# Maxima of the second pair in two rows, another rate of maxima in the first pairs, and routing and list operands in fewer instructions set further apart

## The chip, the cores and the metric

The kernel runs on one core of one Trainium2 chip. The metric is device time in microseconds of one execution. A core has a matrix engine (PE, with its weight loads PEld), a vector engine (DVE), an activation engine (ACT), a general engine (POOL) and a queue engine (SP) that here only issues transfers. Each of them works through its own queue in order. Matmuls write to PSUM, which DVE and ACT empty; POOL cannot read PSUM.

## The reference

Attention with pairs of queries averaged, then a mixture of eight experts in which each token goes to one expert.

```python
B, H, S, D = 8, 8, 1152, 64
q_pool = q.reshape(B, H, S // 2, 2, D).mean(axis=3)            # 576 queries a head
scores = 1 / sqrt(D) * q_pool @ k.T
attn = exp(scores - scores.max(-1)); attn /= attn.sum(-1) + 1e-9
x = (attn @ v) as (4608 tokens, 512)
logits = x @ w_gate + modality_bias[modality_id]               # 8 experts
e_idx = argmax(logits); gate_w = softmax(logits)[e_idx]
for e in range(8):
    mask = e_idx == e
    out[mask] = gate_w[mask] * (relu(x[mask] @ w1[e]) @ w2[e]) # 512 -> 1024 -> 512
```

## The kernel before, in words

**Attention.** 64 heads are taken as 32 pairs p (two batches of one head number). A pair is 18 steps t (`NSTEP`), so attention is 576 steps, and the order of every engine's queue (PE, ACT, DVE, POOL) is written by the loop over t: `ORD` says for each step, in turn modulo three, which generators move on. `s` advances the scores of a third of a head (four banks of 432 columns, two matmuls each, L833 and L834, an exponential on ACT, L835, tile Pe). `v` advances the products with the values (L886 to L888, tile xp), which trail by `LAG` steps. `M` and `X` advance the maxima pass (`maxpass`) of a later pair: PE multiplies a block of 128 queries by 512 keys into a PSUM tile pm (L771), DVE reduces it to one column of mp (L772); the last 128 keys of up to four blocks share one tile (L779, L780). When all nine blocks of 128 queries are done, `row` reduces mp to nine columns (m9, L743), PE turns them (L747), DVE scales them (mr, L756) and SP copies them as one row into B2 (L757), where the scores find them. `maxpass` has 21 stops and a last turn that ends it, 22 turns. `M` comes three times in three steps, `X` once per step: it gives three turns before step `T_F` = 7, one in each step up to 53, then one in every fourth step, or one whenever two passes are queued. Pair 1's pass is queued at step `T_M1`, pair p's at `T_MAX` = -24 before its own first step, for pair 2 six steps later (`D2`).

For each pair the queue also carries: the sum of the query halves (rawq, POOL, L603), the high and low fp16 parts of queries and keys (qh, hi, lo), their copies into QB, B1 and B2 (SP), the low parts Pl of the exponentials (L816 on ACT, L818 on DVE, two thirds on one and one third on the other; `LOWS_LIST` gives ACT some more in pairs 26 to 30), the power of two that scales the values (`power`, `scales`: half, sc and the two scale tiles scales and both, L696 and L698), the scaled values VH (L725, POOL from pair 2 on), VS (L735, DVE), vl (L723), the result of a head (rs, rr, x, L904 to L909) and its split for the gate's logits. `V1`, `T_P1`, `T_P2`, `D2` place such work of pairs 1 and 2.

**Routing.** After every eighth pair one of four token groups g has its logits. `route(g)` is a generator of small instructions on DVE and POOL: the one-hot of the best expert, its gate, and with ten small matmuls each token's position in its expert. `yield n` lets n steps pass. It stands in the list `side`, which moves at the end of a step. After group 2 the generator `first_list` makes the list of the first six blocks of 256 tokens: `first_blocks` (which expert owns a block), `place` (row of each token), `listing` with `operands` (DVE builds ol, o and r for nine tiles of tokens in three portions, PE multiplies them, L498). At step 557 whatever is left of it is run at once (`gather_first`), and POOL gathers the first rows. In steps that are not forced the generator waits `SLOW` = 3 steps between portions.

**Experts.** Blocks of 256 tokens, weights split into two fp16 parts, three products each; group 3's route and the second list run beside them, one `yield` per eighth of a product.

Of the kernel before, what the change touches and what calls it, by code (L numbers as in the profile page):

```python
# [13 lines left out]
I32 = mybir.dt.int32  # L14
# [29 lines left out]
RS = 2  # L44
# [27 lines left out]
V1 = (7, 9, (12, 13), 14, (14, 15))  # L72
# [70 lines left out]
T_PRE = 2  # L143
# [11 lines left out]
class Router:  # L155
# [11 lines left out]
    def setup(self, ids, w_gate, bias):  # L167
        nc, con = self.nc, self.con
        wg = con.tile([P, 4, E], F32, name="wg")
        nc.sync.dma_start(out=wg, in_=w_gate.rearrange("(c p) e -> p c e", p=P))  # L170
        self.wg = con.tile([P, 4, 3, E], BF16, name="wg3")
        for i in range(3):
            nc.gpsimd.tensor_copy(self.wg[:, :, i], wg)
            if i < 2:
                nc.gpsimd.tensor_tensor(wg, wg, self.wg[:, :, i], op=ALU.subtract)
        self.b0 = con.tile([P, 2, E], F32, name="bias")
        nc.sync.dma_start(out=self.b0, in_=bias.rearrange("m e -> (m e)").unsqueeze(0).broadcast_to([P, 2 * E]).rearrange("p (m e) -> p m e", m=2))
        idt = con.tile([P, NTT, 2], I32, name="idt")
# [10 lines left out]
        self.ie = self.iota("ie", E)  # L189
        self.lane16 = con.tile([P, P], BF16, name="lane16")  # L190
# [76 lines left out]
    def route(self, g, eng):  # L267

        nc, sm = self.nc, self.sm
# [20 lines left out]
        yield RS  # L290
# [6 lines left out]
        yield RS  # L297
        oh = big[1][:, 1]
        nc.vector.tensor_tensor(oh, key, bc(kmin), op=ALU.is_equal)
        oh16 = sm.tile([P, NT, E], BF16, name="oh16")  # L300
        nc.vector.tensor_copy(oh16, oh)
        nc.vector.tensor_single_scalar(self.exp[:, ts], kmin, float(E), op=ALU.add)
        yield RS
        sx = sm.tile([P, NT], F32, name="sx")
        nc.vector.tensor_reduce(sx, w, op=ALU.add, axis=AX.X)
        nc.vector.tensor_single_scalar(sx, sx, EPS, op=ALU.add)
# [3 lines left out]
        nc.vector.tensor_single_scalar(ts2[:, 0:1], ts2[:, 0:1], 1.0 / XSC, op=ALU.mult)  # L310
# [5 lines left out]
        yield RS  # L316
# [102 lines left out]
    def place(self, nt, late):  # L419
# [23 lines left out]
        if late:  # L443
# [18 lines left out]
        nc.vector.tensor_copy(self.hi, ri)  # L462
        nc.vector.tensor_single_scalar(self.hi, self.hi, -float(2 * T // P), op=ALU.add)

    def operands(self, g, n, out):

        nc, sm = self.nc, self.sm
        for q in range(3):
            ts = slice(g * NT + 3 * q, g * NT + 3 * q + 3)
            ol = sm.tile([P, 3, P], BF16, name=f"ol{q}", bufs=1 + self.lag)  # L470
            nc.vector.tensor_tensor(ol, self.lo[:, ts].unsqueeze(2).broadcast_to([P, 3, P]), self.lane16.unsqueeze(1).broadcast_to([P, 3, P]),
                                    op=ALU.is_equal)
            yield SLOW
            o = sm.tile([P, 3, n], F32, name=f"o{n}")
            r = sm.tile([P, 3, 2, n], BF16, name=f"r{n}_{q}", bufs=1 + self.lag)
            nc.vector.tensor_tensor(o, self.hi[:, ts].unsqueeze(2).broadcast_to([P, 3, n]), self.col[:, 0:n].unsqueeze(1).broadcast_to([P, 3, n]),
                                    op=ALU.is_equal)
            nc.vector.tensor_tensor(r[:, :, 0], o, self.tile1[:, ts].unsqueeze(2).broadcast_to([P, 3, n]), op=ALU.mult)
            nc.vector.tensor_scalar(r[:, :, 1], o, self.part, None, op0=ALU.mult)
            out.append((ol, r))  # L480
            yield SLOW

    def listing(self, groups, n, acc):

        nc, ops = self.nc, []
        for g in range(groups + self.lag):
# [52 lines left out]
def attention(tc, ctx, att, ident, npairs, xpool, on_two, on_split, on_scale, jobs, side, set_pm, started, ahead, hip):  # L539
# [153 lines left out]
    def scales(p, pt):  # L693
# [66 lines left out]
    def maxpass(p, mp=None):  # L760
# [3 lines left out]
        u0 = 0 if mp is None else 5  # L764
        rest = []
        if mp is None:
            mp = sm.tile([P, 9, 3], F32, name="mp")
        for u in range(u0, 9):
# [6 lines left out]
            if len(rest) == 4 or u == 8:  # L775
# [5 lines left out]
                rest.clear()  # L781
                yield
# [13 lines left out]
    def scores(p, j, r):  # L796
# [10 lines left out]
        lows = LOWS_LAST if p == npairs - 1 else LOWS_LIST if p >= P_LIST else LOWS if p else LOWS0  # L807
# [12 lines left out]
        for t in range(4):  # L820
            need(p, *(("place", "row9") if p else ("row9",) if j else ("row5",)))
# [191 lines left out]
    for p in range(npairs):  # L1013
        b = NSTEP * p
        go = lambda t, f, *a, p=p, b=b, **k: at(b + t, p, lambda: f(p, *a), **k)
        if p > 1:
# [8 lines left out]
            go(T_MAX + d[4], lambda p: mxq.append(maxpass(p)), end=False)  # L1025
# [31 lines left out]
    for t in range(NSTEP * npairs):  # L1057
# [4 lines left out]
        for a in ORD[t % len(ORD)]:  # L1062
# [6 lines left out]
            elif a == "X":  # L1069
                advance(mxq, 3 if t < T_F else 1 if t < 54 or t % 4 == 0 or len(mxq) > 1 else 0)  # L1070
# [410 lines left out]
```

## Time and profile before

| | us |
|---|---|
| median of three runs (lowest, highest) | 1164.33 (1164.32, 1165.66) |
| the profiled execution's own time | 1162.89 |
| its span | 1161.2 |
| PE busy | 1109.2 |
| DVE busy | 986.0 |
| ACT busy | 920.7 |
| POOL busy | 414.0 |
| granted PE clock over the span | 0.996 |

Rows of the profile name the line, the engine, the operation, what is written and read, and the shapes. In a list of waits the columns are the total in us, how often, and the longest. In the rows in order of time the first number is the start and the second the length, in us from the start of the span; x3 means three instructions in a row, and a bracket gives idle time ahead of it and what ended it. A matmul's end is modelled, and successive ones overlap.

### The profile page before, as it was taken

What the parts mean: (1) busy time and instruction counts of PE and PEld (TensorE: products, weight loads), DVE (VectorE), ACT (ScalarE), POOL (GpSimd) and SP (SyncE); (2) the same over time, 40 slices, a digit from 0 to 9 for tenths busy, and PEclk for the clock granted to TensorE, in tenths of its full rate; (3) what the DMA queues carried; (4) which work ended last, traced back from release to release, by engine and by line L of the source; (5) the groups of instructions that cost most, each with busy time, mean ns of one, the idle gap of its engine ahead of it and who ended that gap; (6) DMA issues with size and microseconds to landing.
All of it is one profiled execution on the core that took longest, in us unless ns stands there. A gap on an engine that the chain in (4) does not pass through costs nothing. (4 is left out here: it accounts for less than half of the span.)

```text
span 1161.2 us, 36622 instructions
## 1 busy us (share of the span) xinstructions
PE 1109.2 (96%) x14962; PEld 814.1 (70%) x14962; DVE 986.0 (85%) x2021; ACT 920.7 (79%) x1469; POOL 414.0 (36%) x394
## 2 busy tenths in 40 slices
PE   5989999999999999999999999999999999999995
PEld 2767777777777777777777677767676676766763
DVE  6888999999999999999999999788997667566671
ACT  5879999998999998999999999866566656565561
POOL 7843443444435344444443342123122121221201
PEclk9999999999999999999999999999999999999998
DMA  7667758767668668678678563599989999999970
GB/s 226 171 167 171 175 159 203 166 166 184 162 166 193 175 165 179 165 165 195 160 174 183 144 139 85 173 291 267 254 283 280 322 263 278 281 280 287 269 227 22
DMA packets 175569, 232.66 MB, mean 200 GB/s; under 512 B 92351, under 2 KB 126799, under 8 KB 175392
## 3 DMA queue, kind: packets, MB, share of 16 engines
q1 hardware_dynamic: 169254, 210.45, 70.3%
q0 software_dynamic: 6128, 19.78, 6.0%
q8 instruction: 119, 1.95, 0.7%
q14 instruction: 58, 0.48, 0.1%
q10 hardware_dynamic: 10, 0.00, 0.0%
HBM read 146.11 MB, written 19.18 MB: 142 GB/s over the span
## 5 line engine op out<-in xcount | busy, mean ns | idle before, releaser
L835 ACT ACTIVATE Pe<-psc 128x432 int32<-128x432 f32 x768 | 379.1, 526 | 51.7 <-PE psc L834 42.7
L772 DVE TENSOR_REDUCE mp<-pm 128x1 f32<-128x512 f32 x566 | 370.9, 683 | 18.4 <-PE pm L771 11.4
L886 PE MATMUL xp<-VH,Pe 128*128 128x65 f16 x2880 | 373.2, 193 | 0.0
L888 PE MATMUL xp<-VS,Pl 128*128 128x65 f16 x2880 | 372.5, 193 | 0.4 <-DVE Pl L818 0.4
L887 PE MATMUL xp<-vl,Pe 128*128 128x64 f16 x2880 | 371.2, 192 | 0.0
L887 PEld LDWEIGHTS <-Pe 128*128 128x128 f16 x2880 | 267.6, 98 | 87.8
L834 PE MATMUL psc<-B 65*128 65x432 f16 (+2 forms) x1152 | 305.6, 288 | 4.6 <-DMA B<-mr 4.3
L886 PEld LDWEIGHTS <-Pe 128*128 128x128 f16 x2880 | 272.1, 98 | 52.6 <-issue 15.3
L833 PE MATMUL psc<-B 128*128 128x432 f16 (+2 forms) x1152 | 305.0, 287 | 3.3 <-ACT Pe L835 3.0
L888 PEld LDWEIGHTS <-Pl 128*128 128x128 f16 x2880 | 266.5, 97 | 0.6 <-DVE Pl L818 0.5
L816 ACT ACTIVATE Pl<-Pe 128x1152 f16<-128x1152 uint16 x196 | 223.3, 1140 | 6.2
L771 PE MATMUL pm<-hi,QB 128*128 128x512 f16 x566 | 215.2, 382 | 11.7 <-DVE mp L772 8.3
L725 POOL TENSOR_SCALAR VH<-rawv,sc 128x512 f16<-128x512 f32 (+1 forms) x60 | 103.9, 1742 | 174.1 <-PE psc L834 72.8
L638 POOL TENSOR_TENSOR lo<-rawk,hi 128x576 f16<-128x576 f32 (+1 forms) x68 | 87.4, 1288 | 187.3 <-ACT hi L622 144.4
L1222 PE MATMUL ph<-xpart,w1l 128*128 128x256 f16 x544 | 148.3, 273 | 0.0
L1220 PE MATMUL ph<-xpart,w1h 128*128 128x256 f16 x544 | 148.3, 273 | 0.0
L1221 PE MATMUL ph<-xpart,w1h 128*128 128x256 f16 x544 | 148.3, 273 | 0.0
L834 PEld LDWEIGHTS <-B 65*128 65x128 f16 x1152 | 113.1, 98 | 28.6 <-issue 5.3
L833 PEld LDWEIGHTS <-B 128*128 128x128 f16 x1152 | 112.8, 98 | 8.2 <-issue 3.0
L1226 DVE SCALAR_TENSOR_TENSOR hl<-ph,hh 128x512 f16<-128x512 f32 x72 | 49.6, 689 | 74.5 <-ACT hh L1225 74.4
L1268 PE MATMUL po<-w2h,hl 128*128 128x512 f16 x296 | 112.2, 379 | 0.0
L1267 PE MATMUL po<-w2l,hh 128*128 128x512 f16 x296 | 112.2, 379 | 0.0
(264 smaller groups left out, 1843.3 us busy)
## 6 DMA issues: line engine op xcount, KB each, us to landing
w2r<-in_w_dram SPq DMA_DIRECT2D x76, 512.0 KB
w1r<-in_w_dram SPq DMA_DIRECT2D x72, 512.0 KB
rawv<-in_att_dram SPq DMA_DIRECT2D x32, 576.0 KB
B<-hi SPq DMA_DIRECT2D x128, 144.0 KB
rawq<-in_att_dram SPq DMA_DIRECT2D x31, 576.0 KB
rawk<-in_att_dram SPq DMA_DIRECT2D x31, 576.0 KB
B<-qh SPq DMA_DIRECT2D x128, 72.0 KB
B<-lo SPq DMA_DIRECT2D x64, 144.0 KB
```

What stands on the lines that cost most here:

```text
L771: nc.tensor.matmul(pm, QB[p % 2][:, u], s["hi"][:, t * 512:(t + 1) * 512], start=True, stop=True)
L772: nc.vector.tensor_reduce(mp[:, u, t:t + 1], pm, op=ALU.max, axis=AX.X)
L816: nc.scalar.activation(low, rest, AF.Copy, scale=LOW)
L833: nc.tensor.matmul(o, b1[:, ks], b1[:, qs], start=True, stop=False, skip_group_check=True)
L834: nc.tensor.matmul(o, b2[:, ks], b2[:, qs], start=False, stop=True, skip_group_check=True)
L835: nc.scalar.activation(Pe[:, D + x0:D + x1], pt, AF.Exp, scale=1.0 / 16)
L886: nc.tensor.matmul(out, Ph[:, qs], vh[:, c, j, 0:D + 1], start=c == 0 and g == 0, stop=False, skip_group_check=True)
L887: nc.tensor.matmul(out[:, 0:D], Ph[:, qs], vl[:, c, j], start=False, stop=False, skip_group_check=True)
L888: nc.tensor.matmul(out, Pl[:, qs], vs[:, c, j, 0:D + 1], start=False, stop=c == NKC - 1, skip_group_check=True)
L1220: nc.tensor.matmul(o, hi[:, c, fs], xh[:, :, c], start=c == 0, stop=False)
L1221: nc.tensor.matmul(o, hi[:, c, fs], xl[:, :, c], start=False, stop=False)
L1222: nc.tensor.matmul(o, lo[:, c, fs], xh[:, :, c], start=False, stop=c == 3)
```

## The change

It has five parts.

1. Maxima in the first pairs. `X` gives one turn in each step only up to step 7, then in every third step to step 104 and in every fourth after that. Three turns instead of two are taken ahead of the loop (`T_PRE`). Pair 1 (`TWO_ROWS`) makes its row in two pieces, of five and four blocks, so that its first head's scores need only the first. Pair 2's pass is queued at step 13 instead of 18, pair 3's at 31 instead of 30. The inputs of pair 2 move 2 to 3 steps forward (`D2`, `T_P2`), pair 1's copies 2 forward (`T_P1`) and its values 2 to 4 back (`V1`), the set-up of the router one step forward (`T_RT`).
2. scales and both are copied from sc by POOL one step later (`keep`) instead of computed by DVE.
3. `route`: two DVE instructions become one (key), the one-hot is written as bf16 at once, the cast goes, and the expert number and two scalings go to POOL. Groups 0 and 1 wait four steps between portions instead of two (`RS`), and three short waits are added.
4. `first_blocks` and `place` let a step or two pass after nearly every instruction; the product with TB is folded into the one before it.
5. `operands` builds o and r for nine tiles in one instruction each instead of three; ol stays in three. `LOWS_LIST` gives ACT its extra third in pairs 26 and 27 only, and DVE that of pairs 28 to 30.

The diff's core ("..." where rows are left out):

```diff
-RS = 2
+PL = 2
+RS = (4, 4, 2, 2)
-P_LIST = 26
+P_LIST = {26: 0, 27: 0}
-T_RT = 25
-D2 = (4, 2, 2, 3, 6)
+T_RT = 24
+D2 = (1, 0, 0, 0, 3)
-T_P2 = 4
-T_P1 = 7
+T_P2 = 1
+T_P1 = 5
-V1 = (7, 9, (12, 13), 14, (14, 15))
+V1 = (9, 11, (14, 15), 18, (18, 19))
-T_PRE = 2
+T_PRE = 3
+TWO_ROWS = (1,)
+X_ALL = 8
+X_SOME = 105
+X_IN = 3
+T_MX2 = -23
+T_MX3 = -23
...
     def route(self, g, eng):
-        nc.vector.tensor_single_scalar(w2, lg, 0.0, op=ALU.is_ge)
-        nc.vector.scalar_tensor_tensor(key, w2, -float(E), be(self.ie), op0=ALU.mult, op1=ALU.add)
+        nc.vector.scalar_tensor_tensor(key, lg, 0.0, be(self.ieE), op0=ALU.is_ge, op1=ALU.mult)
...
-        oh = big[1][:, 1]
+        oh = sm.tile([P, NT, E], BF16, name="oh16")
         nc.vector.tensor_tensor(oh, key, bc(kmin), op=ALU.is_equal)
-        nc.vector.tensor_copy(oh16, oh)
-        nc.vector.tensor_single_scalar(self.exp[:, ts], kmin, float(E), op=ALU.add)
-        yield RS
+        yield 1
+        nc.gpsimd.tensor_scalar(self.exp[:, ts], kmin, float(E), None, op0=ALU.add)
+        yield rs
         nc.vector.tensor_reduce(sx, w, op=ALU.add, axis=AX.X)
-        nc.vector.tensor_single_scalar(sx, sx, EPS, op=ALU.add)
         nc.vector.tensor_reduce(ts2[:, 0:1], self.scales[g].bitcast(F32), op=ALU.max, axis=AX.X)
-        nc.vector.tensor_single_scalar(ts2[:, 0:1], ts2[:, 0:1], 1.0 / XSC, op=ALU.mult)
+        yield 1
+        nc.gpsimd.tensor_scalar(sx, sx, EPS, None, op0=ALU.add)
+        nc.gpsimd.tensor_scalar(ts2[:, 0:1], ts2[:, 0:1], 1.0 / XSC, None, op0=ALU.mult)
+        yield 1
         nc.vector.reciprocal(ts2[:, 1:2], ts2[:, 0:1])
...
     def operands(self, g, n, out):
+        rows(0)
+        yield SLOW
+        nc.vector.tensor_tensor(o, self.hi[:, ts].unsqueeze(2).broadcast_to([P, NT, n]), ..., op=ALU.is_equal)
+        yield SLOW
+        rows(1)
+        yield SLOW
+        nc.vector.tensor_tensor(r[:, 0], o, self.tile1[:, ts].unsqueeze(2).broadcast_to([P, NT, n]), op=ALU.mult)
+        nc.vector.tensor_scalar(r[:, 1], o, self.part, None, op0=ALU.mult)
+        yield SLOW
+        rows(2)
+        yield SLOW
...
     def scales(p, pt):
-        on_scale(p, lambda o: power_of(o, half, 1, 49))
+        later(1, lambda: keep(p, sc))
+    def keep(p, sc):
+        on_scale(p, lambda o: nc.gpsimd.tensor_copy(o, sc[:, 1:2]))
-        power_of(st[p - p % 2]["both"][r], half[r], 1, 49)
+        nc.gpsimd.tensor_copy(st[p - p % 2]["both"][r], sc[r, 1:2])
...
     def maxpass(p, mp=None):
-            if len(rest) == 4 or u == 8:
+            if len(rest) == 4 or u == 8 or two and u == 4:
+                if two and u == 4:
+                    later_end(FIN if now[0] > NSTEP else 1, row(p, mp, 0, 5))
...
-                advance(mxq, 3 if t < T_F else 1 if t < 54 or t % 4 == 0 or len(mxq) > 1 else 0)
+                advance(mxq, 3 if t < T_F else 1 if t < X_ALL or t % (X_IN if t < X_SOME else 4) == 0 or len(mxq) > 1 else 0)
```

How instructions move on DVE during pair 1, between two low parts Pl (L818 before, L862 now; three steps lie between two of them). Reductions of maxima are L772 and L780 before, L813 and L821 now. Before:

```order
L818 TENSOR_SCALAR Pl_120<-Pe_119 128x576
L772 TENSOR_REDUCE mp<-pm 128x1 x2
L780 TENSOR_REDUCE mp<-pm 128x4
L772 TENSOR_REDUCE mp<-pm 128x1 x3
L818 TENSOR_SCALAR Pl_122<-Pe_121 128x576
```

And after:

```order
L862 TENSOR_SCALAR Pl_120<-Pe_119 128x576
L813 TENSOR_REDUCE mp<-pm 128x1 x4
L862 TENSOR_SCALAR Pl_122<-Pe_121 128x576
```

Six reductions stood in these three steps, and four stand there now.

On DVE in the route of group 0, the part around the one-hot and the gate (half, sc, scales and both belong to the pair's own value scale). Before:

```order
L780 TENSOR_REDUCE mp<-pm 128x4
L696 TENSOR_SCALAR half<-pm 128x1
L698 TENSOR_SCALAR sc<-half 128x1 x2
L698 TENSOR_SCALAR scales<-half 128x1
L698 TENSOR_SCALAR both<-half 64x1
L299 TENSOR_TENSOR wide_5691<-wide_5691,kmin 128x72
L301 CAST oh_5987<-wide_5691 128x72
L302 TENSOR_SCALAR exp<-kmin 128x9
L772 TENSOR_REDUCE mp<-pm 128x1 x2
L818 TENSOR_SCALAR Pl_116<-Pe_115 128x576
L305 TENSOR_REDUCE sx<-wide_5690 128x9
L306 TENSOR_SCALAR sx<-sx 128x9
```

After, from the same one-hot (now L306) on:

```order
L306 TENSOR_TENSOR oh_6230<-wide_5702,kmin 128x72
L813 TENSOR_REDUCE mp<-pm 128x1
L821 TENSOR_REDUCE mp<-pm 128x1
L783 TENSOR_REDUCE m_6301<-mp 128x9
L906 SCALAR_TENSOR_TENSOR x_5661<-x_5214,sc,x_5660 128x9x64
L862 TENSOR_SCALAR Pl_122<-Pe_121 128x576
L796 TENSOR_SCALAR mr<-pm 9x128
L813 TENSOR_REDUCE mp<-pm 128x1
L948 TENSOR_SCALAR rs<-xp 128x5
```

The one-hot now stands alone among the pair's own work, and the sum of the gate (L311, eight rows further on) comes after other reductions.

On POOL in an undisturbed pair. Before:

```order
L638 TENSOR_TENSOR lo<-rawk,hi 128x576 x2
L603 TENSOR_TENSOR rawq<-rawq 128x576
L725 TENSOR_SCALAR VH_127<-rawv,sc 128x8x64
L725 TENSOR_SCALAR VH_127<-rawv,sc 128x10x64
L610 CAST qh<-rawq 128x576
```

After:

```order
L674 TENSOR_TENSOR lo<-rawk,hi 128x576 x2
L744 COPY scales<-sc 128x1
L746 COPY both<-sc 64x1
L639 TENSOR_TENSOR rawq<-rawq 128x576
L765 TENSOR_SCALAR VH_123<-rawv,sc 128x8x64
L765 TENSOR_SCALAR VH_123<-rawv,sc 128x10x64
```

The two copies, which read DVE's sc, stand ahead of the sum of the query halves and of VH.

More of the change, by code (lines that the diff above doesn't have):

```diff
@@ L52 @@
 LOWS_LAST = (((0, 864, 'D', 1), (864, 1728, 'D', 3)),)
-P_LIST = 26
-LOWS_LIST = (((0, 1152, 'A', 2), (1152, 1728, 'D', 3)), ((0, 1152, 'A', 2), (1152, 1728, 'D', 3)), ((0, 1152, 'A', 2), (1152, 1728, 'A', 3)))
+P_LIST = {26: 0, 27: 0}
+LOWS_LIST = [tuple(((0, 1152, 'A', 2), (1152, 1728, e, 3)) for e in x) for x in ('DDA', 'DA', 'A')]
 D0 = 5
-T_RT = 25
-D2 = (4, 2, 2, 3, 6)
+T_RT = 24
+D2 = (1, 0, 0, 0, 3)
 T_K2 = 0
 T_F = 7
-T_P2 = 4
-T_P1 = 7
+T_P2 = 1
+T_P1 = 5
 T_M1 = 5
@@ L189, in setup @@
         self.ie = self.iota("ie", E)
+        self.ieE = self.iota("ieE", E, base=-E)
         self.lane16 = con.tile([P, P], BF16, name="lane16")
@@ L289, in route @@
         nc.vector.tensor_tensor(lg, lg, bc(mx), op=ALU.subtract)
[L290 removed]
+        yield rs
         nc.scalar.activation(w, lg, AF.Exp)
[L292 removed]
         key = big[1][:, 0]
[L294 removed]
+        nc.vector.scalar_tensor_tensor(key, lg, 0.0, be(self.ieE), op0=ALU.is_ge, op1=ALU.mult)
         kmin = sm.tile([P, NT], F32, name="kmin")
         nc.vector.tensor_reduce(kmin, key, op=ALU.min, axis=AX.X)
[L297 to L298 removed]
+        yield rs
+        oh = sm.tile([P, NT, E], BF16, name="oh16")
         nc.vector.tensor_tensor(oh, key, bc(kmin), op=ALU.is_equal)
[L300 to L303, printed above, removed]
+        yield 1
+        nc.gpsimd.tensor_scalar(self.exp[:, ts], kmin, float(E), None, op0=ALU.add)
+        yield rs
         sx = sm.tile([P, NT], F32, name="sx")
         nc.vector.tensor_reduce(sx, w, op=ALU.add, axis=AX.X)
[L306 removed]
         gt = sm.tile([P, NT, 2], F32, name="gt")
@@ L366, in first_blocks @@
         full = self.con.tile([P, E], F32, name="full")
-        self.up_to(self.base, full)
+        i = sm.tile([P, E], I32, name="cnti")
+        nc.vector.tensor_copy(i, self.base)
         yield
-        cum = self.running(full.unsqueeze(1), "cumA")[:, 0]
+        nc.vector.tensor_single_scalar(i, i, TB.bit_length() - 1, op=ALU.logical_shift_right)
+        yield
+        nc.vector.tensor_copy(full, i)
+        yield
+        w = sm.tile([P, 1, E + 1, E], F32, name="wcumA")
+        nc.vector.tensor_tensor(w[:, 0], full.unsqueeze(1).broadcast_to([P, E + 1, E]), self.before, op=ALU.mult)
+        yield
+        cum = self.con.tile([P, E + 1], F32, name="cumA")
+        nc.vector.tensor_reduce(cum, w[:, 0], op=ALU.add, axis=AX.X)
         yield
@@ L372, in first_blocks @@
         nc.vector.tensor_scalar(left, cum[:, 0:E], -1.0, float(NA), op0=ALU.mult, op1=ALU.add)
+        yield
+        cut = self.con.tile([P, E + 1], F32, name="cutA")
         nc.vector.tensor_single_scalar(left, left, 0.0, op=ALU.max)
+        nc.vector.tensor_single_scalar(cut, cum, float(NA), op=ALU.min)
+        self.cumA = cut
+        yield
         self.na = self.con.tile([P, E], F32, name="na")
         nc.vector.tensor_tensor(self.na, full, left, op=ALU.min)
+        c3 = sm.tile([P, NA, E], F32, name="own3A")
+        nc.vector.tensor_tensor(c3, self.col[:, 0:NA].unsqueeze(2).broadcast_to([P, NA, E]), cut[:, 1:].unsqueeze(1).broadcast_to([P, NA, E]), op=ALU.is_ge)
         yield
-        nc.vector.tensor_single_scalar(cum, cum, float(NA), op=ALU.min)
-        self.cumA = cum
+        ef = sm.tile([P, NA], F32, name="ownA")
+        nc.vector.tensor_reduce(ef, c3, op=ALU.add, axis=AX.X)
         yield
-        self.ownA = self.owners(cum, NA, "A")
+        self.ownA = self.con.tile([P, NA], I32, name="ownerA")
+        nc.vector.tensor_single_scalar(self.ownA, ef, float(E - 1), op=ALU.min)
     def other_blocks(self):
@@ L449, in place @@
             nc.vector.tensor_tensor(row, row, more, op=ALU.add)
+        nc.vector.tensor_tensor(ok, self.pos[:, 0:nt], lim, op=ALU.is_ge if late else ALU.is_lt)
         yield
-        nc.vector.tensor_tensor(ok, self.pos[:, 0:nt], lim, op=ALU.is_ge if late else ALU.is_lt)
         nc.vector.scalar_tensor_tensor(row, row, float(2 * T), ok, op0=ALU.add, op1=ALU.mult)
@@ L455, in place @@
         nc.vector.tensor_copy(ri, row)
-        lo = sm.tile([P, NTT], I32, name="loi")[:, 0:nt]
+        yield
+        lo, hi = (sm.tile([P, NTT], I32, name=f"{x}i")[:, 0:nt] for x in ("lo", "hi"))
         nc.vector.tensor_single_scalar(lo, ri, P - 1, op=ALU.bitwise_and)
-        nc.vector.tensor_single_scalar(ri, ri, 7, op=ALU.logical_shift_right)
+        nc.vector.tensor_single_scalar(hi, ri, 7, op=ALU.logical_shift_right)
+        yield
         self.lo = sm.tile([P, NTT], BF16, name="lof")[:, 0:nt]
@@ L467, in operands, with rows @@
         nc, sm = self.nc, self.sm
[L468 to L471, printed above, removed]
-                                    op=ALU.is_equal)
[L473 to L481, printed above, removed]
+        ts = slice(g * NT, (g + 1) * NT)
+        r = sm.tile([P, 2, NT, n], BF16, name=f"r{n}", bufs=1 + self.lag)
+        ols = [sm.tile([P, 3, P], BF16, name=f"ol{q}", bufs=1 + self.lag) for q in range(3)]
+        out.append((ols, r))
+        def rows(q):
+            t3 = slice(g * NT + 3 * q, g * NT + 3 * q + 3)
+            nc.vector.tensor_tensor(ols[q], self.lo[:, t3].unsqueeze(2).broadcast_to([P, 3, P]), self.lane16.unsqueeze(1).broadcast_to([P, 3, P]),
+                                    op=ALU.is_equal)
+        rows(0)
+        yield SLOW
+        o = sm.tile([P, NT, n], F32, name=f"o{n}")
+        nc.vector.tensor_tensor(o, self.hi[:, ts].unsqueeze(2).broadcast_to([P, NT, n]), self.col[:, 0:n].unsqueeze(1).broadcast_to([P, NT, n]),
+                                op=ALU.is_equal)
+        yield SLOW
[6 more added lines that the diff above has]
+        yield SLOW
     def listing(self, groups, n, acc):
@@ L496, in listing @@
                 for t in range(NT):
-                    ol, r = ops[g][t // 3]
-                    nc.tensor.matmul(pm, ol[:, t % 3], r[:, t % 3], start=t == 0, stop=t == NT - 1)
+                    ols, r = ops[g][0]
+                    nc.tensor.matmul(pm, ols[t // 3][:, t % 3], r[:, :, t], start=t == 0, stop=t == NT - 1)
                 yield 1
@@ L764, in maxpass @@
         u0 = 0 if mp is None else 5
+        two = p in TWO_ROWS
         rest = []
@@ L820, in scores @@
         for t in range(4):
-            need(p, *(("place", "row9") if p else ("row9",) if j else ("row5",)))
+            need(p, *(("place",) if p else ()), "row5" if j == 0 and (p == 0 or p in TWO_ROWS) else "row9")
             pt = ps_sc.tile([P, 512], F32, name="psc")[:, 0:BANK]
@@ L1024, in attention @@
                 go(T_LO[LOCI[i] if LOC else i] + d[3], split_lo, i)
-            go(T_MAX + d[4], lambda p: mxq.append(maxpass(p)), end=False)
+            go({2: T_MX2, 3: T_MX3}.get(p, T_MAX), lambda p: mxq.append(maxpass(p)), end=False)
             go(T_PLACE + (T_P2 if p == 2 else 0), place, end=False)
```

27 lines of the change are left out of this document (14 added, 13 removed).

## The prediction

> **What bounds the kernel now.** I read the page's busy shares first. Every engine name below is the page's.
>
> ```profile
> PE 1109.2 (96%) x14962; PEld 814.1 (70%) x14962; DVE 986.0 (85%) x2021; ACT 920.7 (79%) x1469; POOL 414.0 (36%) x394
> ```
>
> PE is busy 96% of the span, so only the 52 us in which it is not can be won. To see where they lie I cut the span at the starts of the reciprocal of head 0 (L905), one per pair, and read busy time by stretch. Columns: stretch, length, then busy us (instructions) of PE, PEld, DVE, ACT, POOL, then the granted clock, the DMA share and GB/s.
>
> ```profile
> 20.00:43.44 23.44, 21.60 (x258) 14.10 (x257) 20.49 (x48) 22.15 (x37) 16.73 (x12) 1.00 0.70 214
> 43.44:68.07 24.63, 21.72 (x370) 16.25 (x367) 20.88 (x44) 19.75 (x33) 20.16 (x36) 1.00 0.64 156
> 68.07:94.61 26.54, 22.73 (x372) 17.16 (x371) 21.84 (x46) 20.93 (x36) 8.06 (x6) 1.00 0.77 165
> 94.61:116.92 22.31, 21.83 (x388) 16.96 (x385) 20.74 (x45) 20.21 (x35) 8.78 (x8) 1.00 0.58 155
> 205.85:249.62 43.77, 43.77 (x761) 33.95 (x760) 42.34 (x92) 41.72 (x72) 20.56 (x20) 1.00 0.73 178
> 249.62:296.05 46.43, 44.58 (x771) 34.38 (x770) 44.65 (x109) 42.39 (x73) 19.48 (x17) 1.00 0.69 168
> 428.38:474.79 46.41, 44.56 (x771) 34.35 (x770) 44.63 (x109) 42.40 (x73) 19.48 (x17) 1.00 0.70 169
> 607.87:656.24 48.37, 45.35 (x773) 34.63 (x772) 47.19 (x125) 44.28 (x76) 20.05 (x17) 1.00 0.68 161
> 656.24:704.87 48.63, 45.53 (x772) 34.83 (x771) 47.68 (x117) 45.19 (x76) 19.56 (x15) 1.00 0.55 124
> 770.00:1140.00 370.00, 370.00 (x2599) 249.88 (x2598) 267.83 (x408) 221.66 (x284) 76.47 (x71) 1.00 0.95 271
> ```
>
> The fifth row is the yardstick: two undisturbed pairs take 43.77 us, PE never idle, so a pair costs 21.9 us and PE sets it. DVE stands 1.43 us for the two pairs, 0.7 per pair: it is nearly as full. The last row is the expert stage: PE idle nowhere, so nothing that DVE does there counts. Against the yardstick too much time goes in three places: the first pairs (24.63 + 26.54 + 22.31 = 73.48 against 65.7, 7.8 us), the two lone routes (2.66 and 2.64 us), and four pairs with the third route and the list (48.37 + 48.63 = 97.00 against 87.5, 9.5 us). Together 22.6 us. Then I asked whom PE waited for.
>
> ```profile
> PE pm L771 <- DVE mp L772: 8.3, 14, 1.1
> PE psc L834 <- DMA B<-mr: 4.3, 7, 1.2
> PE pm L747 <- DVE m L743: 3.9, 7, 1.2
> PE psc L833 <- ACT Pe L835: 3.0, 5, 1.5
> PE pm L779 <- DVE mp L772: 1.7, 3, 0.7
> PE pm L771 <- DMA QB<-qh: 1.3, 1, 1.3
> ```
>
> Columns: us in total, times, longest. L771 and L779 are the maxima pass, whose PSUM buffers DVE empties; L747 turns the row of maxima. So PE, which works in order, stands mainly because DVE's queue is behind. Waits of L834 on the row's transfer recur in undisturbed pairs too; no part of the change aims at them.
>
> **The change, part by part.** First the price of a DVE instruction, from one route (start, length, instruction):
>
> ```profile
> 254.78 1.88 DVE L772 TENSOR_REDUCE mp<-pm 128x1 f32<-128x512 f32 x3
> 256.57 0.45 DVE L818 TENSOR_SCALAR Pl<-Pe 128x576 f16<-128x576 uint16 x1
> 256.94 0.68 DVE L780 TENSOR_REDUCE mp<-pm 128x4 f32<-128x512 f32 x1
> 257.86 0.14 DVE L698 TENSOR_SCALAR scales<-half 128x1 int32<-128x1 int32 x1
> 258.01 0.15 DVE L698 TENSOR_SCALAR both<-half 64x1 int32<-64x1 int32 x1
> 258.18 0.64 DVE L299 TENSOR_TENSOR wide<-wide,kmin 128x72 f32<-128x72 f32 x1
> 258.85 0.20 DVE L301 CAST oh<-wide 128x72 bf16<-128x72 f32 x1
> 258.96 0.17 DVE L302 TENSOR_SCALAR exp<-kmin 128x9 f32<-128x9 f32 x1
> 259.04 1.28 DVE L772 TENSOR_REDUCE mp<-pm 128x1 f32<-128x512 f32 x2
> 260.86 0.17 DVE L306 TENSOR_SCALAR sx<-sx 128x9 f32<-128x9 f32 x1
> 260.94 0.15 DVE L309 TENSOR_REDUCE ts<-scales 128x1 f32<-128x8 f32 x1
> 261.13 0.15 DVE L310 TENSOR_SCALAR ts<-ts 128x1 f32<-128x1 f32 x1
> 261.31 0.16 DVE L311 RECIPROCAL ts<-ts 128x1 f32<-128x1 f32 x1
> ```
>
> Starts tell more than lengths. Three maxima take 256.57 - 254.78 = 1.79, so 0.60 each; the low part (Pl) 0.37. An instruction that uses the one before it starts after its end (L310 to L311: 0.18), one that does not starts before that end (L302 to the maxima: 0.08). Spacing a chain out is thus worth about 0.1 us a link.
>
> *First pairs.* Between two Pl of DVE lie three steps, a sixth of a pair: 21.9 / 6 = 3.65 us of PE time. An undisturbed sixth holds 3.5 reductions of maxima (21 a pair, L772 and L780) and DVE is busy 42.34 / 43.77 of it, 3.53 us. A sixth with six needs 3.53 + 2.5 x 0.60 = 5.03, 1.4 more than PE's. In pairs 1 and 2 before, six of seven successive sixths hold six and one holds three: 6 x 1.4 - 0.4 = 8.0 us of backlog, close to the 7.8 seen. The sixths beside these hold none to three, and there DVE runs dry. Now nearly all of them hold three or four (the reductions go on at 4 per three steps, where steps 8 to 53 had 6): a sixth with four needs 3.83, 0.18 too much, over some 12 of them 2.2 us, less 0.3 a pair for the two scale writes taken off DVE (257.86 to 258.18), so about 1.5 us remain. The second row of maxima for pair 1 adds one transpose, two small DVE instructions (0.18 and less each) and one transfer, in sixths that have room. Gain 7.8 - 1.5 = 6.3. Pair 0 (20.00 to 43.44) might give up some of its 1.84 us of PE idle, but ACT is busy 22.15 of its 23.44 us, so I take nothing. Pair 2's row has less margin: its pass needs 22 turns; at 6 per three steps from step 18 it was done at step 29, at 4 per three from step 16 it is done at 32, four steps (4.9 us) ahead of its scores at 36. I take 0.3 off: **6.0 us**, ends 0 and 9.6 (7.8 + 1.84).
>
> *Lone routes.* DVE loses scales and both (0.32), the cast and the expert number (258.85 to 259.04: 0.19), two scalings (0.08 and 0.18) and one comparison (like L310, 0.2): 1.0 us of the cluster, and the rest is spread over twice the steps, so the 2.6 us of stall, made by one cluster, should nearly go. What stays is PE's own work, ten instructions more than in the yardstick (771 against 761): their busy time is 0.81 us, but successive matmuls overlap in it. The gain of one route lies between the idle time, 46.43 - 44.58 = 1.85, and the whole 2.66; I take **2.1 each, 4.2**, ends 0 and 5.3. Three results now come from POOL; DVE's reciprocal, which the maxima queue behind, waits for two of them, one step (1.2 us) later. POOL had been idle 1.94 us before its own copy there (row below), so no wait is charged; were it in a burst, up to 3.43 us per route.
>
> *List.* The rows of one third of a group:
>
> ```profile
> 677.25 0.18 DVE L476 TENSOR_TENSOR o<-hif,col 128x36 f32<-128x36 f32 x1
> 677.46 0.20 DVE L478 TENSOR_TENSOR r<-o,tile 128x36 bf16<-128x36 f32 x1
> 677.57 0.24 DVE L479 TENSOR_SCALAR r<-o,part 128x36 bf16<-128x36 f32 x1
> 677.74 0.68 DVE L772 TENSOR_REDUCE mp<-pm 128x1 f32<-128x512 f32 x1
> ```
>
> A group had three such threes, 3 x 0.49 = 1.47 us; now one three of triple width. Width costs (0.68 - 0.18) / (512 - 36) = 1.05 ns an element, from L772 and L476, so 72 elements more in each of three are 0.23 and the triple 0.72: 0.75 saved a group, less a little for added waits, 0.7; that is 1.4 for the two groups before 704.87. The route saves 0.7, scales and both 4 x 0.3 = 1.2, spacing some 10 links of first_blocks and place 1.0; two Pl of pair 28 come back to DVE from ACT, 2 x 0.37 = 0.7 lost. Sum 3.6; the stalls fall by about what the backlog falls, and smaller clusters help: **4.0 us**, ends 0 and 9.5. Pairs 29 and 30 get four Pl more on DVE (1.5) and save about that. List and blocks end some 11 steps later in program order, yet still at the drain ahead of the first gather, which holds as many list instructions as before.
>
> *Scale copies on POOL.* In every pair two copies go ahead of POOL's add of the query halves and wait for DVE's sc; the add ran early before.
>
> ```profile
> 206.70 1.41 POOL L603 TENSOR_TENSOR rawq<-rawq 128x576 f32<-128x576 f32 x1
> 213.77 3.43 POOL L725 TENSOR_SCALAR VH<-rawv,sc 128x512 f16<-128x512 f32 x2 [5.67 <-PE xp L888]
> 220.47 0.45 DVE L735 TENSOR_SCALAR VS<-VH 128x1152 f16<-128x1152 f16 x1
> 258.04 1.56 POOL L725 TENSOR_SCALAR VH<-rawv,sc 128x512 f16<-128x512 f32 x1 [6.17 <-PE pm L771]
> 261.55 0.19 POOL L314 COPY gt<-ts 128x9 f32<-128x9 f32 x1 [1.94 <-DVE ts L311]
> ```
>
> So VH moves back by 1.41 + 2 x 0.19 = 1.8 us; VS on DVE started 220.47 - 217.20 = 3.3 us after VH, and that margin covers it. Cost nothing; ends 0 and +4 us.
>
> The Trainium skill (SBUF — State Buffer, Who interferes with whom) states that a DVE instruction with two SBUF inputs and a GpSimd one that reads SBUF take a shared port pair as an exclusive lock, so the later blocks until the first ends. By it L299, begun at 258.18 beside the VH of 258.04, would have waited until 259.60; the trace has it done at 258.82, so it shows less than a full block. By the rule, 62 copies of 0.19 us would cost DVE at most 12 us over all pairs, 0.4 a pair, and the time would come out at 1154, since some ten pairs have DVE behind.
>
> In undisturbed pairs 0.4 is less than the 0.7 us that DVE stands, so the sum stays.
>
> **Sum.** 6.0 + 4.2 + 4.0 = 14.2 us; the expert stage and the rest of the pairs unchanged. The profiled execution took 1162.89 (span 1161.2, 1.7 around it), 1.4 below the median of 1164.33. From the median: 1164.3 - 14.2 = 1150.1, so **1150**.
>
> **Rivals.**
> The first pairs do not gain: pair 2's row, four steps ahead, or pair 3's QB, still behind POOL's set-up, is late in the place of DVE. For it: the 1.3 us wait on QB now. Against: it is one wait of 1.3 among 7.8. Time 1164.3 - 8.2 = 1156.
> No change: ACT, busy 92 to 95% of these stretches, stops PE as soon as DVE does not. Against: PE's waits on ACT are 3.0 us in all. Time 1163.
> Slower: VH comes too late in every pair. If the two copies, or the wait for sc, hold POOL 3.3 us instead of 1.8, DVE's VS waits, and the maxima behind it. DVE has 1.0 us to spare (0.7 + 0.3), so it decides from a shift of about 4.3 us; each further us costs one in some 28 pairs. At 5.3 us, with 14 gained: 1164 + 28 - 14 = 1178.
>
> **How the numbers follow.** The forecast as a whole gets 0.60, the first rival 0.22, no change 0.08, slower 0.10. The forecast's own range is 1144 (start 7.8, routes 5.3, list 7) to 1154. Two in ten left out on the outer sides, the range is 1143 to 1161. About 0.2%, 2.3 us, is what a measurement of this kernel can tell. Faster 0.83 (the first two and a little of the third), same 0.07, slower 0.10.
>
> **What would show it.** Pairs 0 to 3 near 22 us each, sixths with four maxima; the two stretches with lone routes near 44.5; the four list pairs near 93; PE's wait on mp of L771 under 3 us; VS on DVE waiting for nothing; the expert stage as long as before. A wait of DVE on VH or on POOL's ts2, of PE on QB or mr in the first pairs, or ACT as PE's main releaser, would make it wrong.

## The result: 1179.10 us, 1.2% slower

The changed kernel takes 1179.10 us (median of 4, 1177.84 to 1180.81), the kernel before 1164.78 beside it; the ratio is 1.0123, with a 95% interval of 1.0105 to 1.0141. The forecast was 1150. Ratios here go by fast runs alone; one run of e7 below was slow, 2185 us at a granted clock of 0.884, and is left out of its ratio. The profiled execution spans 1178.0 us, against 1161.2 before. Its page's busy shares:

```profile
PE 1111.1 (94%) x14963; PEld 815.6 (69%) x14963; DVE 989.8 (84%) x1897; ACT 924.1 (78%) x1463; POOL 438.1 (37%) x472
```

DVE has 124 instructions fewer and is yet busy 3.8 us longer: some of its instructions have become slower. Where the time went, by stretches as before (stretch, length, busy us of PE, PEld, DVE, ACT, POOL). Each stretch starts at the instruction just ahead of a head-0 reciprocal (L948 and L949 now, 0.17 us apart). As in the prediction, pair 0 is what lies ahead of the first of them, and the first row here is pair 1:

```profile
43.25:62.73 19.48, 19.07 (x349) 14.95 (x344) 18.64 (x39) 16.71 (x29) 16.48 (x38) 1.00 0.57 155
62.73:86.84 24.11, 22.82 (x384) 17.45 (x385) 23.25 (x47) 21.90 (x38) 11.41 (x11) 1.00 0.72 189
86.84:110.34 23.50, 22.31 (x390) 17.20 (x389) 21.23 (x45) 21.16 (x36) 10.12 (x10) 1.00 0.76 170
341.89:365.03 23.14, 21.99 (x373) 16.90 (x372) 22.23 (x44) 21.36 (x37) 9.98 (x10) 1.00 0.62 164
365.03:388.40 23.37, 22.22 (x390) 17.19 (x389) 21.09 (x46) 21.24 (x36) 9.97 (x10) 1.00 0.81 171
249.57:296.12 46.55, 44.73 (x772) 34.40 (x771) 44.55 (x101) 42.69 (x73) 21.77 (x25) 1.00 0.71 168
626.75:723.88 97.13, 90.09 (x1532) 69.06 (x1531) 93.27 (x219) 87.64 (x148) 41.91 (x42) 1.00 0.62 142
```

Pairs 1 to 3 now take 67.1 us instead of 73.5; here the gain is there. But the undisturbed pairs (rows four and five, pairs 14 and 15) take 46.5 for two instead of 43.8, the lone route with its pair as much as they, and the four list pairs 97.1 as before. From pair 5 to pair 25 the kernel loses 24 us, and that is the result: +24.0 there, -5.0 up to pair 4, about -2 behind pair 25, together 16.8, the difference of the spans. The list of PE's waits shows whom it stands for (us in total, times, longest):

```profile
PE pm L812 <- DVE mp L813: 18.0, 29, 1.7
PE psc L878 <- DMA B<-mr: 14.9, 13, 2.7
```

They were 8.3 (14 times) and 4.3 (7 times) before. Now the instructions of pair 16, first as before has it on POOL and DVE, then after (start, length):

```profile
392.02 3.44 POOL L725 TENSOR_SCALAR VH<-rawv,sc 128x512 f16<-128x512 f32 x2 [5.67 <-PE xp L888]
395.40 0.67 POOL L610 CAST qh<-rawq 128x576 f16<-128x576 f32 x1
396.15 1.28 POOL L638 TENSOR_TENSOR lo<-rawq,qh 128x576 f16<-128x576 f32 x1
400.10 1.61 POOL L638 TENSOR_TENSOR lo<-rawk,hi 128x576 f16<-128x576 f32 x1 [2.67 <-ACT hi L622]
398.72 0.45 DVE L735 TENSOR_SCALAR VS<-VH 128x1152 f16<-128x1152 f16 x1
399.69 0.88 DVE L723 SCALAR_TENSOR_TENSOR vl<-rawv,sc,VH 128x640 f16<-128x640 f32 x1
```

```profile
396.47 0.19 POOL L744 COPY scales<-sc 128x1 int32<-128x1 int32 x1 [7.07 <-DVE sc L734]
396.72 0.18 POOL L746 COPY both<-sc 64x1 int32<-64x1 int32 x1
396.98 1.41 POOL L639 TENSOR_TENSOR rawq<-rawq 128x576 f32<-128x576 f32 x1
398.37 3.64 POOL L765 TENSOR_SCALAR VH<-rawv,sc 128x512 f16<-128x512 f32 x2
401.96 0.66 POOL L646 CAST qh<-rawq 128x576 f16<-128x576 f32 x1
402.71 1.38 POOL L674 TENSOR_TENSOR lo<-rawq,qh 128x576 f16<-128x576 f32 x1
404.60 1.27 POOL L674 TENSOR_TENSOR lo<-rawk,hi 128x576 f16<-128x576 f32 x1 [0.51 <-ACT hi L658]
402.87 1.54 DVE L775 TENSOR_SCALAR VS<-VH 128x1152 f16<-128x1152 f16 x1
404.93 1.62 DVE L763 SCALAR_TENSOR_TENSOR vl<-rawv,sc,VH 128x640 f16<-128x640 f32 x1
```

VS waits for nothing. It starts 0.16 us after a POOL subtraction (lo) and takes 1.54 us instead of 0.45, to 0.3 us behind the end of that lo; vl, beside the next lo, takes 1.62 instead of 0.88. Before, VS stood in a gap of POOL of 2.67 us. Counted from half (391.52 before, 396.01 after) the first lo came 2.1 us later and met VS; the second lo did not move (8.6 us behind half in both), and vl was pushed onto it by the long VS. In the changed kernel VS is over 0.6 us in 9 of 31 pairs, before in none. Over the whole execution the groups of the page say the same (busy, mean ns), first before, then after:

```profile
L735 DVE TENSOR_SCALAR VS<-VH 128x1152 f16<-128x1152 f16 x31 | 14.1, 455 | 1.2 <-ACT VH L727 1.2
L723 DVE SCALAR_TENSOR_TENSOR vl<-rawv,sc,VH 128x640 f16<-128x640 f32 (+1 forms) x60 | 51.1, 851 | 0.0
```

```profile
L775 DVE TENSOR_SCALAR VS<-VH 128x1152 f16<-128x1152 f16 x31 | 23.8, 769 | 0.0
L763 DVE SCALAR_TENSOR_TENSOR vl<-rawv,sc,VH 128x640 f16<-128x640 f32 (+1 forms) x60 | 57.6, 960 | 0.0
L813 DVE TENSOR_REDUCE mp<-pm 128x1 f32<-128x512 f32 x566 | 374.1, 684 | 35.5 <-PE pm L812 29.5
```

The maxima (L813), which read PSUM, are not touched: 0.67 to 0.69 us each, beside POOL's work or not. The Trainium skill (SBUF — State Buffer, Who interferes with whom) has the rule: a DVE copy, cast or tensor_scalar can enter a two-port mode, contends there with GpSimd for the shared port pair, and whoever issues first blocks the other for the whole instruction; reductions don't enter it. The rows of VS and of the maxima agree. Beside VH the traces show a shorter block. The prediction showed L299, 72 columns, at 0.64 us, begun 0.14 us behind the start of VH. The same line runs a fourth time in the trace of before, with no arithmetic on POOL beside it:

```profile
780.25 0.23 DVE L299 TENSOR_TENSOR wide<-wide,kmin 128x72 f32<-128x72 f32 x1
```

So VH held L299 up by 0.41 us and not, as that rule has it, for the 1.4 us that it had still to go.

In odd pairs the loss has another face: the row. SP's queue of pair 16 and the start of 17, before and after:

```profile
396.09 1.11 SPq L573 DMA_DIRECT2D QB<-qh  x2
402.02 5.25 SPq L870 DMA_TRANSPOSE xt<-x  x2
407.37 0.80 SPq L757 DMA_DIRECT2D B<-mr  x1
```

```profile
402.65 2.04 SPq L609 DMA_DIRECT2D QB<-qh  x2
408.39 5.50 SPq L914 DMA_TRANSPOSE xt<-x  x2
413.98 0.79 SPq L797 DMA_DIRECT2D B<-mr  x1
```

Counted from half, the copies of qh leave 4.6 us later before and 6.6 after, the row 15.9 and 18.0: POOL's late qh holds SP's queue up by 2 us, and the row stands at its end, behind two transposes. That is not the whole of it: one transpose holds the queue for 1.2 to 3.3 us before (median 2.0) and for 1.3 to 4.2 after (2.4), so the row's place varies by more than qh does.

### The profile page after: what moved, and what is told of

It reads as the page before. It is cut to its first block, busy times and chain, and to the rows that moved or that the text cites. A ratio compares the mean times of both kernels' runs of the same rounds, so it can differ in the third digit from the quotient of the medians.

```text
span 1178.0 us, 36598 instructions
## 1 busy us (share of the span) xinstructions
PE 1111.1 (94%) x14963; PEld 815.6 (69%) x14963; DVE 989.8 (84%) x1897; ACT 924.1 (78%) x1463; POOL 438.1 (37%) x472
## 5 line engine op out<-in xcount | busy, mean ns | idle before, releaser
L879 ACT ACTIVATE Pe<-psc 128x432 int32<-128x432 f32 x768 | 384.9, 527 | 67.8 <-PE psc L878 57.0
L813 DVE TENSOR_REDUCE mp<-pm 128x1 f32<-128x512 f32 x566 | 374.1, 684 | 35.5 <-PE pm L812 29.5
L860 ACT ACTIVATE Pl<-Pe 128x1152 f16<-128x1152 uint16 (+1 forms) x190 | 219.6, 1156 | 6.0
L1310 PE MATMUL po<-w2h,hh 128*128 128x512 f16 x296 | 112.2, 379 | 0.0
```

What stands on the lines that cost most here:

```text
L813: nc.vector.tensor_reduce(mp[:, u, t:t + 1], pm, op=ALU.max, axis=AX.X)
L860: nc.scalar.activation(low, rest, AF.Copy, scale=LOW)
L879: nc.scalar.activation(Pe[:, D + x0:D + x1], pt, AF.Exp, scale=1.0 / 16)
```

## The experiments

**e1 to e4: which part.** The theory is that the two POOL copies wait for sc ahead of POOL's query add and so move VH, qh and the first lo by 2 us, into VS on DVE, and VS pushes vl into the second; the rivals, that each copy costs by itself, or that the loss lies in the rates, routes or list.

e1, the changed kernel with these two writes on DVE again:

```diff
-        later(1, lambda: keep(p, sc))
+        on_scale(p, lambda o: power_of(o, half, 1, 49))
+        power_of(st[p - p % 2]["both"][r], half[r], 1, 49)
```

> The changed kernel with the two scale tiles written by DVE again, as before; all else of the change stays. Theory (the POOL copies stand ahead of the query add, shift VH and qh by about 2 us, and so make VS and vl run beside POOL's lo): VS back at 0.45 us and the 640-wide vl at 0.88 in every pair, ordinary pairs back from 23.5 to 22.4 us each, in all 1179 - 28 x 1.1 = 1148 us, between 1145 and 1155. Rival (the new rate of maxima, the routes or the list cost the time): stays above 1170.

1155.09 us, ratio to before 0.9921 (0.9895 to 0.9947). Even pairs (mean of 12, 14, 16, 20, 22, 24) are back at 21.64 us, where the changed kernel has 23.07; VS is 0.45 in 28 of 31. So 24 us hang on which engine runs two instructions, of 0.19 us each on POOL.

e2, the copies on POOL but behind VH, qh and the first two lo:

```diff
-        later(1, lambda: keep(p, sc))
+        later(10 if p > 1 else 1, lambda: keep(p, sc))
```

> The changed kernel with the same two POOL copies per pair, issued nine steps later, behind the query add, VH, qh and the first two lo of POOL. Theory (what counts is the shift, not the copies): VH starts 0.5 us after half again instead of 2.1 to 2.4, VS 0.45 us, and the time falls to 1145 to 1152 us, at or a little under the kernel with the DVE writes, which has 0.3 us more DVE work a pair. Rival (each copy on POOL costs DVE by itself, through waiting for sc or through the port it uses): stays above 1165.

1158.73 us, 0.9945 (0.9924 to 0.9967), 6.7 us above the expected range. Even pairs take 21.57, so the copies themselves cost nothing there; the odd ones (13, 15, 17, 21, 23, 25) 23.47, and PE waits 11.6 us in all on the row, against 5.2 in e1. The copies of qh leave 4.85 us behind half there, so a late row does not need a late qh. Some 20 of the 24 us are in the place, not in the copies; that e2 lies 3.6 above e1, with intervals that overlap, is not explained.

e3, the kernel before with `keep` alone, as in the changed kernel.

> The kernel before with one edit alone: the two scale tiles are copied on POOL one step behind sc, ahead of the query add, instead of written on DVE. Theory: the ordinary pairs of the changed kernel appear, 23.4 us each with VS at 1.54 us in every other pair, so 1164 + 28 x 1.1 = 1195 us, between 1185 and 1200. Rival (the copies are harmless, the loss lies in other parts): 1164 or less, since DVE has two instructions fewer in a pair.

1193.69 us, 1.0247 (1.0213 to 1.0282), as worked out: even pairs 23.14, VS at 1.54 in 11 of 31.

e4, the kernel before with the first pairs' part alone (`X_ALL`, `X_SOME`, `X_IN`, `TWO_ROWS`, `T_PRE`, `T_MX2`, `T_MX3`, `D2`, `T_P1`, `T_P2`, `V1`, `T_RT`).

> The kernel before with the first pairs' part of the change alone (rates of maxima, two rows for pair 1, shifted inputs of pairs 1 to 3). Theory: the gain that the changed kernel shows at its start, 5.0 to 7.6 us by pair 4, is kept to the end: 1157 to 1160 us. Rival 1 (the gain is given back in later pairs through late rows): 1164. Rival 2 (the new rate is what slows the pairs): above 1170.

1153.82 us, 0.9902 (0.9874 to 0.9930): more than expected. By the start of pair 5 it leads by 8.6 us (129.82 against 138.37), and ends 7.9 ahead by the spans. Since e1 holds this part and routes and list too, and is no faster than e4, those two together gained nothing that shows.

**e5 and e9: the row.** e5 is the changed kernel with `XL = 4` instead of 3, which puts the row between the two transposes.

> The changed kernel with the second transpose of x (and its split on DVE) one step later, so that on SP's queue the row mr goes out between the two transposes of an odd pair instead of behind both; VH, qh and lo stay as late as in the changed kernel. Theory (the late POOL costs twice: in even pairs by VS and vl beside lo, in odd pairs by a late SP queue, at whose end the row stands): PE's wait on the row, 14.0 us in 11 odd pairs, falls under 4, the even pairs stay at 23.1 us with VS at 1.54, in all 1166 to 1170 us. Rival (the row is late because loads crowd the transfers, wherever it stands in the queue): 1177 to 1181.

1193.67 us, 1.0237 (1.0208 to 1.0267): the wait fell as expected and the time rose against it. PE's waits of e5:

```profile
PE pm L812 <- DVE mp L813: 31.9, 48, 2.3
PE psc L878 <- DMA B<-mr: 2.8, 6, 0.9
```

The row's wait was in the queue, then; but the split of x, 0.81 us on DVE, moved as well, and VS, vl and Pl met POOL more often (VS over 0.6 us in 13 of 31 pairs, the 640-wide vl over 1 us in 20 of 30). e9 makes the same edit on e1.

> The kernel with the scale tiles written by DVE (e1), and the second transpose of x with its DVE split one step later, so that the row goes out ahead of it on SP. In the changed kernel this took PE's wait on the row away (14.0 to 2.5 us) and yet lost 14 us, because DVE then ran VS, vl and Pl beside POOL more often. Theory (it is the place of DVE's port-locking instructions against POOL's that decides, and e1 has VS clear of lo by over a microsecond): the row's wait falls from 4.7 to under 2 us, VS stays at 0.45, 1155 - 3 = 1152 us. Rival (the shift of the split by itself costs DVE or PE): 1160 or more, with the wait on mp of L809 up.

1167.34 us, 1.0023 (1.0008 to 1.0037): the rival. In the profiled execution, the slowest of ten (1172.95 us), the row's wait is 2.1 us, VS is at 0.45 in 28 of 31, and yet even pairs rise to 22.35 and PE waits 38 times on mp instead of 14. So 12 us are the price of moving the split by a step, by a way that these runs don't show, and e5 doesn't tell what the row alone cost.

**e6 and e7: the port by itself.** The kernel before; POOL gets useless work in the 2.67 us in which VS had run alone, and no result of it is used. e6 subtracts, e7 only writes:

```diff
+        if p > 1 and i == 0:
+            for _ in range(2):
+                nc.gpsimd.tensor_tensor(idle, t[:, r], h[:, r], op=ALU.subtract)   # e6
+                nc.gpsimd.memset(idle, 0.0)                                        # e7
```

> The kernel before with two useless POOL subtractions per pair (1.28 us each, both inputs in SBUF, result used by nobody), behind the first lo, where POOL was idle for 2.6 us; they fill just the gap in which VS ran alone, and nothing that SP waits for moves. Theory (the lock of the shared port by itself): VS rises from 0.45 to between 1.2 and 1.6 us in most pairs, and even pairs go from 21.64 to between 22.5 and 23.2 us; with odd pairs absorbing part, 1164 + 12 to 30, about 1180 us. Rival (VS was slow for another reason, as the order of its own queue): VS stays 0.45, 1164 us.

> The same gap of POOL filled by two useless memsets of about the same length, which write SBUF and read nothing. If the lock is on the pair of ports as a whole: VS as slow as with the subtractions, 1.2 to 1.6 us, about 1180 us. If only reads of SBUF by POOL collide with DVE: VS stays 0.45 us and the time 1164.

1208.73 us, 1.0360 (1.0325 to 1.0395), and 1208.46 us, 1.0365 (1.0326 to 1.0404). e7's group of VS, and one VS with POOL beside it:

```profile
L738 DVE TENSOR_SCALAR VS<-VH 128x1152 f16<-128x1152 f16 x31 | 41.7, 1344 | 1.2 <-ACT VH L730 1.2
...
421.40 1.65 DVE L738 TENSOR_SCALAR VS<-VH 128x1152 f16<-128x1152 f16 x1
...
419.83 2.90 POOL L641 MEMSET idle<- 128x1472 f16 x2
```

VS starts 0.2 us into the second memset and ends 0.3 us behind it. The copies of qh leave 4.57 us behind half as before, and the next lo starts when it did (e6) or at most 0.14 us later (e7). So the stretching, of VS and of the vl that VS pushes onto that lo (1.29 us), costs 44 us, more than the 29 of e3; VS is over 0.6 us in 24 and 23 of 31 pairs here, in 11 there. That POOL reads nothing does not help VS.

**e8, e10, e11: where the list's gain went.** In e1 the instructions of list and third route are fewer on DVE (56 against 78 in pairs 26 to 30) and yet hold DVE's queue for 18.0 us, start to start, against 18.9. Three of them, with POOL's instruction beside the first:

```profile
640.69 1.46 DVE L451 TENSOR_TENSOR wide<-exp,ie 128x216 f32<-128x216 f32 x1
672.86 1.07 DVE L508 TENSOR_TENSOR o<-hif,col 128x108 f32<-128x108 f32 x1
684.98 1.42 DVE L502 TENSOR_TENSOR ol<-lof,lane 128x384 bf16<-128x384 bf16 x1
```

```profile
639.95 1.97 POOL L674 TENSOR_TENSOR lo<-rawk,hi 128x576 f16<-128x576 f32 x1 [3.24 <-ACT hi L658]
```

They take 0.37, 0.25 and 0.55 where POOL stands. Each reads two operands from SBUF. First e8 tried the simpler cause, the four Pl that `LOWS_LIST` gives back to DVE: e1 with the table of before.

> The changed kernel with the scale tiles written by DVE and, besides, the shares of the low parts in pairs 26 to 30 as before (ACT takes the extra third in all five). Theory (the list part lost where it gave DVE four more Pl in pairs 29 and 30): pair 29 falls from 25.5 to about 23.6 us, the others of the five stay, 1155 - 2 = 1153 us. Rival (pair 29 is late because the list itself ends later): 25.5 stays and 1155 or more.

1154.20 us, 0.9916 (0.9883 to 0.9950); pair 29 stays at 25.3 us, so these Pl alone were not its cause. e10 is e1 with routes and list going on only in the steps that meet POOL's gaps, with shorter waits between them:

```diff
-PL = 2
-RS = (4, 4, 2, 2)
+PL = 1
+RS = (2, 2, 1, 2)
-SLOW = 3
+SLOW = 1
+FREE = (0, 1, 6, 9, 10, 11, 14, 15, 16, 17)
...
-        if side and t >= wait:
+        if side and t >= wait and c18 in FREE:
```

> The kernel with the scale tiles written by DVE (e1), whose routes and list go forward only in those ten of the 18 steps of a pair after which POOL stands idle in the trace, one instruction group per such step, so that they still end in the same pair. In e1 the route and list instructions of pairs 26 to 30 stretched by some 6.6 us beside POOL (1.46 us for a 0.37 one), which ate the 5 us that the fewer and wider instructions save. Theory (the shared port took that gain): stretching there falls to under 3 us, the five pairs from 119.9 to 115 to 117 us, in all 1151 us. Rival (the list is late for DVE's sheer amount of work): the five pairs stay at 119 or more.

1155.37 us, 0.9920 (0.9894 to 0.9945): half right. These instructions, 60 now, hold DVE for 16.0 us (L451's successor takes 0.37), the first two list pairs fall to 22.8 each (e1: 23.7 and 24.2), and the lone routes lose next to nothing, 21.98 us for the pair in which they start. But the operands now crowd into pairs 28 and 29:

```profile
647.16:671.58 24.42, 22.33 (x373) 16.98 (x372) 24.04 (x57) 22.61 (x39) 10.03 (x8) 1.00 0.65 148
671.58:698.14 26.56, 24.06 (x406) 18.20 (x405) 26.27 (x60) 22.60 (x37) 10.20 (x8) 1.00 0.41 91
```

DVE is busy 26.27 of 26.56: here the amount of work decides, the rival's case, and the five pairs stay at 119.8. e11 adds the old table of Pl.

> The kernel with routes and list in POOL's gaps (e10), and the shares of the low parts in pairs 26 to 30 as before (four Pl back from DVE to ACT). With the port cleared, DVE is busy 26.27 of 26.56 us in pair 29 of e10, so there the amount of work decides. Theory: pairs 28 to 30 lose 0.4 to 1.0 us each, 1155 - 2 = 1153 us. Rival (ACT, whose share grows, takes over, or one execution's rows on the transfer outweigh it): 1155 or more.

1151.11 us, 0.9894 (0.9870 to 0.9918), a little under the expected 1153; the five pairs fall to 117.0. Up to the list e10 and e11 are the same program, and yet PE waits 10.4 us on the row in the profile of e10 and 5.0 in that of e11: this wait changes from execution to execution.

**e12: the row without moving DVE.** e11, with the rows of odd pairs sent from POOL's queue:

```diff
-            (nc.sync if p or u0 else nc.scalar).dma_start(out=B2[p % 2]...
+            (nc.gpsimd if p > 2 and p % 2 else nc.sync if p or u0 else nc.scalar).dma_start(out=B2[p % 2]...
```

> The same (e11), and the rows of the odd pairs sent from POOL's queue, idle there for some 4 us, instead of from SP's behind the two transposes of x; DVE's order is not touched. Theory (the row waits in SP's queue, and this is worth its wait where no port-locking instruction is moved): PE's wait on the row falls from about 9.7 us to under 3, and the time by 4 to 7 us to 1146 to 1149 us. Rival 1 (the row is late in the transfer engines, not in the queue): no change. Rival 2 (the issue on POOL delays lo, which then meets DVE): 1155 or more, with stretched Pl.

1148.05 us (1146.95 to 1149.40), 0.9854 (0.9829 to 0.9879): the lowest median of all, faster than both kernels. Its interval overlaps that of e11, so the 3 us between the two are not shown. Two pairs with a lone route take half a microsecond more than the yardstick of 43.77 now:

```profile
243.25:287.50 44.25, 44.19 (x771) 34.26 (x770) 43.14 (x105) 41.98 (x73) 21.23 (x22) 1.00 0.74 176
```

PE's wait on the row is 3.3 us, against 5.0 in e11 (the expectation took 9.7, from e10). Whatever gain there is lies under the 4 to 7 us that were expected, and the row still comes late in some pairs.

## Why the prediction was wrong

- **The step that failed** is "Scale copies on POOL", costed at nothing (ends 0 and +4). Its first half was right: VH moved by 1.9 us. "VS on DVE started ... 3.3 us after VH, and that margin covers it" was the error: it asked only whether VS would wait for VH. VS had a second neighbour, POOL's first lo, which moved by 2.1 us onto it, and VS then pushed vl onto the second. VS took 1.54 us instead of 0.45 there. Alone this step costs 29 us (e3).
- **The rule** was weighed, and priced too low. Of L299, 0.64 us beside VH, the prediction said only that it shows less than a full block; with 0.23 us clear of POOL it was a block of 0.41. And the rule was applied only to the copies, 0.19 us each, not to what their shift brings together. The trace of before had the pattern: Pl at 0.95 us beside VH and 0.45 elsewhere.
- **The slower rival** gave 1178, and 1179 was measured, but by another mechanism: VS waits for nothing, at a shift of 1.9 us, where the rival needed 5.3 for this time. That the two numbers meet is luck.
- **First pairs**, 6.0 (0 to 9.6): right in size, and somewhat larger. e4 leads by 8.6 us at pair 5, of which pair 0 has 1.2, which I had taken as nothing; but kernels with the same first part end pair 0 anywhere from 42.3 (e4) to 43.5 us (e8), and before ends it at 43.44, so those 1.2 are not shown. The mechanism is in part argued: the sixths with six reductions are gone, but of the 8.3 us that PE waited at L771 on mp only 0.6 lay ahead of 117 us (5.2 lay behind 600, at the list), and e4 moves rate, rows and inputs together.
- **No change** leant on a list that was short of a row: PE's waits on ACT are 3.0 us only without the 6.8 at L791 on ACT's hi, all in the first 12 us. Nothing in the sum hung on it.
- **Lone routes**, 2.1 each: e1 gains 0.76 (46.43 to 45.67) at the first; in its trace the route pushes the 640-wide vl beside lo (1.70 us, 1.13 before). In e11 the gain is 2.0 (44.41) and in e12 2.2 (44.25). The size was right where the port is clear.
- **List**, 4.0: e1 loses 1.0 (118.84 to 119.82 for pairs 26 to 30). The saving in instructions was there; three rows of e1 show POOL taking 2.8 us of it back. Neither the old Pl alone (e8, 120.2) nor the gaps alone (e10, 119.8) win anything; with both it gains 1.8 (e11).
- **What stays open**: how much of the odd pairs' loss in the changed kernel (24.11 against 22.60 us) is the late row and how much DVE's own lateness, since e5 moved both, and since the wait on the row changes between executions of one program; why e9's split costs 12 us; and why VH blocks DVE for a shorter time than lo does.

## What to carry to other kernels

Before work is moved on GpSimd, or delayed by a wait in its queue, list what DVE does with SBUF operands in the stretch into which everything behind it moves, not only who waits for whom. In a profile, compare the shortest with the mean length of one form of instruction: where they differ, look at what the other engine ran beside the longer ones: here these were blocked, and a wait view did not show it. A chain that is spread out can meet more of the other engine's work; spread it over that engine's gaps.

## What the runs showed of the hardware

- A memset on POOL, which reads nothing, holds VS up as much as a subtraction does: 1.65 us (e7) and 1.54 (changed kernel) for 0.45.
- VH on POOL, 1.56 us long, held a 72-wide instruction of DVE that began 0.14 us behind it up by only 0.41 us (0.64 for 0.23).
- Two POOL copies of 0.19 us ahead of the query add cost 24 us in the changed kernel (e1) and 29 in the one before (e3). Two DMA transposes held SP's queue for 5.25 and 5.50 us in the rows shown; a single one took 1.2 to 4.2 us.
- In e7 a DVE instruction with two SBUF inputs (the split of x) ran its usual 0.81 us beside the memset, for 0.2 us of overlap and in two places only. The Trainium skill (SBUF — State Buffer, Who interferes with whom) says that such an instruction contends only with POOL's reads; this is too little to show it.
